# A new order of all words in an attention-and-gMLP kernel whose schedule is written out by hand

## The chip, the cores and the metric

One Trainium2 chip, one core of it. The time is what the device takes for one execution, in microseconds (us); the profile is one more execution, recorded by the hardware profiler. Engines: PE is TensorE (matmuls; PEld its weight loads), DVE is VectorE, ACT is ScalarE, POOL is GpSimd, SP is SyncE, which here only issues DMAs. A DMA can be issued from SP, ACT or POOL.

## The reference

Attention over 8 batches, 12 heads, 448 positions, head size 64, with q and k normalised by their root mean square, then a gMLP block on the joined heads (768 columns, 1024 hidden):

```python
q_n, k_n = rmsnorm(q, g_q), rmsnorm(k, g_k)
scores = q_n @ k_n.T / sqrt(64)
attn = softmax(scores)
x = (attn @ v) joined over heads          # [8, 448, 768]
h = relu(x @ w_in)                        # [8, 448, 1024]
u, w = h[..., :512], h[..., 512:]
w_n = (w - mean(w)) / sqrt(var(w) + 1e-6) # over the 512
w_s = w_spatial @ w_n + b_spatial         # over the 448 positions
out = (u * w_s) @ w_out                   # [8, 448, 768], float32
```

## The kernel before

The work is cut into words, and one text, `PLAN`, gives the order of all of them by hand. A loop at the end of the kernel reads the text word by word and calls `op_<letter>`. Each engine runs its own words in the order in which they stand, and waits for what another engine has to give. No scheduler changes this order. A word is a name with numbers, then after a slash the numbers of the buffers or PSUM banks it takes, then after a second slash the engine: `a` ACT, `v` DVE, `g` POOL, `s` SP. `E.4.1/c` is the exponential of group 4, unit 1, into buffer 12. PSUM has 8 banks for all uses; `SLOTS` gives the number of the other buffers (10 `raw` for loads, 22 `et`, 5 `os` for output rows).

A group G is four heads of one batch, so a batch has three groups (24 in all), each with seven units. The words in the order of the data:

- `L` loads q (0), k (1) or v (2) of a group, 448 KB, on SP; `l` loads halves of group 0; `gl` the two gains. `w`, `ws`, `wo`, `wb` load the weights, on POOL; `x` copies `w_in` with its rows swapped.
- `Q` squares (ACT, DVE or POOL), `R` sums (DVE), `I` and `J` make 1/rms (ACT), `N` multiplies (POOL or DVE); `q r i j n` are the same for the halves of group 0. `F` casts v.
- `P` and `p` transpose on TensorE and `K`, `k` copy the result from PSUM (DVE or ACT); for groups 6 and up `T` transposes by DMA instead, and `Z` scales k on DVE.
- `S` (L499) makes the scores of a unit on TensorE, eight matmuls on tiles of 64x32 of the array, into two banks; `E` (L507) takes their exponential on ACT.
- `s`, `a`, `b` (L534) are passes over the exponentials: the sums, and the two halves of the product with v; four matmuls of 64x32 for one group, eight when the word does two groups. `D` and `d` invert the sums on ACT, `X` (L563) writes the normalised result on DVE.
- `V` (L579) and `W` (L594) make the gate half of the hidden layer, `c` is its relu; `B`, `M`, `m`, `A` normalise it. `U` (L632) and `u` make the other half. `H` (L647) is the spatial product, `G` (L654) multiplies the halves, `O` (L663) is the output product, `o` (L354, L356) copies it from PSUM, `t` (L679, L681) stores it. `t` of the last 64 rows of two batches (m = 3) stores the pair.
- `z` (L247) is idle work: n matmuls on an identity, whose result nobody reads.

Words of DVE and POOL that read or write large tiles of SBUF go through `port`: each waits for the last such word of the other of the two engines.

Of the kernel before, what the change touches and what calls it, by code (L numbers as in the profile page):

```python
# [27 lines left out]
K.1.1/1/v P.2.0/6 K.2.0/1/v P.1.0/2 K.1.0/2/v s.0.2.0/3 E.0.0/4 S.0.3/45 E.0.3/5 S.0.2/67 E.0.2/6 F.0//g a.0.6.0/0  # L28
N.2.1/3 Q.3.0/1/v s.0.6.0 s.0.3.0 a.0.3.0 a.0.2.0 S.1.4/12 E.1.4/7 Q.4.0/0/v F.1//v s.0.0.0 S.1.6/45 E.1.6/8 S.1.0/67
a.0.1.0 E.1.0/9 S.1.5/12 E.1.5/a S.1.2/45 E.1.2/b R.3.0 P.2.1/6 s.0.4.0 S.1.1/12 E.1.1/c b.0.1.0/7 b.0.4.0 L.7.0/3  # L30
a.0.0.0 s.0.5.0 S.1.3/45 E.1.3/d a.0.4.0 R.4.0 K.2.1/2/v wo w.0 a.0.5.0 s.0.1.0 S.2.6/12 b.0.3.0 s.1.0.0/6 E.2.6/e
Q.3.1/2 R.3.1 I.3 J.3 Q.4.1/1 R.4.1 a.1.3.0/4 b.0.5.0 a.1.1.0 s.1.2.0 I.4 S.2.1/12 E.2.1/f Q.5.0/0 a.1.6.0 s.1.1.0
L.2.2/8 L.5.1/5 L.6.1/0 Y.4/5 s.1.6.0 N.3.1/0/v N.3.0/1/v S.2.0/12 s.1.4.0 s.1.3.0 b.0.6.0 s.1.5.0 L.3.2/9 J.4 N.4.0/2
N.4.1/3 D.0/0 b.1.5.0/3 b.1.6.0 E.2.0/g y.4//v L.7.1/6 a.1.2.0 d.0 S.2.3/12 D.1/1 R.5.0 P.3.1/5 P.3.0/6 K.3.1/3/v
K.3.0/3/v E.2.3/h Y.1/1 y.1//v Y.0/2 y.0//v S.3.4/56 d.1 Q.6.0/2/a a.1.0.0 E.3.4/i a.1.4.0 b.1.0.0 S.3.6/12 E.3.6/j
b.0.2.0 S.3.1/56 E.3.1/k X.0.0 P.4.1/0 Q.5.1/1/v K.4.1/0/v b.1.1.0 S.2.2/12 b.1.4.0 b.1.3.0 E.2.2/l R.5.1 L.4.2/7
S.3.3/56 E.3.3/0 b.0.0.0 b.1.2.0 a.1.5.0 w.1 I.5 X.1.1 X.1.0 Y.2/0 X.0.1 y.2//v S.2.5/12 E.2.5/6 P.4.0/3 K.4.0/0/v
S.3.5/56 E.3.5/2 Y.3/4 y.3//v L.8.0/4 S.3.2/12 Q.6.1/0 R.6.1 F.2//g J.5 R.6.0 E.3.2/8 s.2.1.1/70 s.2.6.1 s.2.3.1
s.2.5.1 F.3//g S.3.0/56 a.2.1.1/34 a.2.6.1 S.2.4/12 L.5.2/8 s.2.2.1 a.2.3.1 E.3.0/9 E.2.4/1 a.2.2.1 s.2.0.1 Q.7.1/1
R.7.1 Q.7.0/0/a R.7.0 N.5.0/0 a.2.5.1 a.2.0.1 S.4.4/56 E.4.4/3 s.2.4.1 b.2.2.1/12 N.5.1/1 a.2.4.1 b.2.3.1 b.2.1.1  # L40
D.2/1 b.2.0.1 b.2.4.1 b.2.5.1 Q.8.0/2 P.5.0/5 K.5.0/2/v L.8.1/9 L.9.1/2 P.5.1/6 K.5.1/1/v I.6 D.3/0 J.6 N.6.1/3 x.2
L.9.0/5 d.2 X.2.0 V.0.2.1/7 I.7 T.6.1/0 V.0.1.1/0 N.6.0/2 T.6.0/3 d.3 b.2.6.1 S.4.1/56 V.0.1.0 V.0.2.0 X.2.1 E.4.1/c
V.0.1.2 Q.9.1/1/a X.3.1 S.5.1/56 E.5.1/7 X.3.0 S.4.0/12 E.4.0/d V.0.2.2 c.0.2//v c.0.1//v R.9.1 V.0.0.1/3 J.7 L.10.0/0
U.0.0.1/4 S.4.6/56 E.4.6/4 S.5.3/12 x.0 U.0.2.2/7 L.11.1/1 B.0.2 Q.8.1/0 U.0.0.2 V.0.0.0 F.5//g E.5.3/5 N.7.0/0/v
Z.6/3/v S.5.2/56 S.5.0/01 E.5.0/b R.8.1 N.7.1/1 T.7.1/1 U.0.0.0 U.0.1.1/2 U.0.1.2 R.8.0 u.0.0//v E.5.2/a S.4.5/01
E.4.5/8 U.0.1.0 S.6.4/56 E.6.4/l U.0.2.1 S.4.3/01 I.8 E.4.3/0 V.0.0.2 u.0.1//v c.0.0//v S.4.2/56 F.4//g Q.9.0/1
E.4.2/h J.8 N.8.1/3 U.0.3.0/4 U.0.3.2 S.5.5/01 E.5.5/f S.5.6/23 E.5.6/k B.0.1 R.9.0 U.0.2.0 U.0.3.1 s.4.0.1/56
S.5.4/01 u.0.3//v E.5.4/9 L.10.1/8 u.0.2//v s.4.2.1 s.4.1.1 T.7.0/1 s.4.6.1 S.6.3/23 E.6.3/g N.8.0/2 s.4.5.1 s.4.3.1
s.4.4.1 D.5/1 b.4.5.1/47 a.4.1.1/01 a.4.0.1 Z.7/2/v a.4.4.1 a.4.5.1 a.4.2.1 a.4.3.1 a.4.6.1 D.4/0 S.6.6/23 b.4.2.1
b.4.6.1 T.8.1/0 d.5 X.5.0 d.4 X.4.0 L.7.2/3 L.6.2/6 T.8.0/0 E.6.6/1 I.9 b.4.1.1 b.4.4.1 b.4.3.1 b.4.0.1 X.5.1 X.4.1  # L50
Q.11.1/0/a S.7.5/56 S.7.3/01 J.9 E.7.3/i V.1.0.0/2 E.7.5/2 V.1.1.2/3 Q.10.0/2 W.0/7 c.0.3//a L.12.1/7 L.11.0/9
Q.10.1/1 S.7.6/01 E.7.6/6 S.7.2/45 E.7.2/e V.1.1.1 V.1.2.1/6 R.11.1 R.10.1 V.1.2.0 B.0.0 V.1.2.2 S.7.0/01 B.0.3
N.9.1/1 T.9.1/1 N.9.0/0 L.15.1/4 L.10.2/2 L.13.0/5 M.0 m.0 Z.8/0/v A.0.3 A.0.0 A.0.2 A.0.1 S.7.4/45 T.9.0/2 V.1.1.0
V.1.0.2 V.1.0.1 E.7.0/j H.0.1/0 c.1.1//a E.7.4/8 c.1.2//a R.10.0 I.10 c.1.0//a H.0.2/1 G.0.2 H.0.3/3 c.1.3//v G.0.3
F.7//a L.12.0/3 S.7.1/45 E.7.1/f S.6.2/12 J.10 Q.11.0/0 F.6//g L.9.2/6 E.6.2/a B.1.2 N.10.0/3 H.0.0/6 G.0.0 L.13.1/0
U.1.1.0/7 U.1.1.1 U.1.1.2 S.6.1/34 E.6.1/h G.0.1 S.6.5/12 u.1.1//a E.6.5/4 S.6.0/56 E.6.0/k O.0.0.1/0 B.1.3 Z.9/1/v
B.1.1 O.0.2.1/3 o.0.2.1/0/a O.0.0.0/4 O.0.2.0/7 o.0.0.1/1/v R.11.0 o.0.2.0//v Q.12.1/1/a U.1.2.2/1 S.9.1/56 I.11 J.11
S.8.0/23 E.8.0/7 B.1.0 R.12.1 Q.15.1/2/a U.1.3.1/0 F.10//g N.10.1/2 T.10.1/0 Q.13.0/0 E.9.1/c O.0.1.0/7 U.1.3.0
U.1.2.0 o.0.0.0//v U.1.3.2 u.1.3//v Q.12.0/1/v M.1 m.1 A.1.2 A.1.3 o.0.1.0/2/v U.1.2.1 U.1.0.2/2 U.1.0.1 U.1.0.0
u.1.2//a u.1.0//a O.0.1.1/3 o.0.1.1//a S.8.5/45 E.8.5/3 x.1 A.1.0 s.6.1.1/06 F.9//v A.1.1 S.9.6/12 E.9.6/9 s.6.0.1  # L60
R.12.0 R.13.0 s.6.3.1 s.6.2.1 N.11.1/1 s.6.5.1 s.6.6.1 s.6.4.1 S.8.2/34 E.8.2/0 Q.13.1/1 H.1.0/7 G.1.0 H.1.1/5 H.1.2/1
D.6/1 S.9.5/23 N.11.0/0 a.6.3.1/40 G.1.2 I.12 D.7/0 G.1.1 J.12 d.6 E.9.5/5 d.7 H.1.3/6 G.1.3 a.6.0.1 N.12.0/2 S.8.4/12
a.6.2.1 E.8.4/b a.6.1.1 a.6.4.1 R.15.1 R.13.1 S.8.1/56 E.8.1/d a.6.6.1 O.1.3.1/7 o.1.3.1/3/v S.9.3/12 b.6.6.1/35
E.9.3/1 b.6.4.1 b.6.2.1 T.10.0/1 L.8.2/2 a.6.5.1 X.7.0 F.8//g N.12.1/3 b.6.0.1 I.13 b.6.5.1 X.6.0 S.8.3/67 b.6.3.1
S.9.4/12 E.9.4/6 b.6.1.1 L.15.0/8 L.12.2/6 O.1.3.0/0 o.1.3.0//v X.6.1 X.7.1 J.13 E.8.3/8 O.1.0.0/4 o.1.0.0/4/a
O.1.0.1/1 o.1.0.1//v S.9.2/67 E.9.2/l Q.15.0/0 s.8.4.1/20 Z.10/2/v L.14.1/1 S.9.0/34 s.8.5.1 s.8.1.1 b.8.5.1/51
s.8.3.1 b.8.1.1 S.8.6/67 E.9.0/a E.8.6/e s.8.2.1 b.8.2.1 b.8.4.1 S.10.1/34 s.8.0.1 b.8.3.1 Q.14.1/2 E.10.1/j t.0.0
T.11.0/3 L.13.2/9 b.8.0.1 L.14.0/3 R.15.0 T.11.1/1 N.13.1/0/v Z.11/3/v s.8.6.1 a.8.5.1/67 a.8.6.1 a.8.0.1 a.8.4.1
D.9/1 F.13//g T.12.1/0 L.16.0/2 t.1.3 b.8.6.1 Q.14.0/1 a.8.1.1 L.16.1/7 D.8/0 a.8.3.1 T.13.1/1 a.8.2.1 S.10.5/34 d.9
X.9.0 d.8 X.8.0 E.10.5/k V.2.1.0/0 V.2.2.1/2 V.2.1.1 L.11.2/0 L.19.1/9 S.11.1/67 E.11.1/2 I.15 J.15 N.15.0/1 V.2.0.1/3  # L70
T.12.0/2 X.9.1 X.8.1 V.2.0.0 S.10.4/45 E.10.4/4 L.15.2/8 S.10.0/67 E.10.0/g V.2.0.2 R.14.1 R.14.0 V.2.1.2 c.2.1//v
c.2.0//v O.1.1.1/1 Q.16.0/0/a S.11.4/45 S.11.0/67 E.11.0/i E.11.4/f I.14 o.1.1.1/1/v V.2.2.0 V.2.2.2 U.2.0.0/0
N.13.0/3/v L.19.0/5 T.13.0/0 Z.13/1/v c.2.2//v U.2.0.1 S.10.6/67 E.10.6/h Z.12/0/v U.2.3.1/3 N.15.1/0 L.17.0/4 R.16.0
S.10.3/45 E.10.3/3 F.11//g S.11.3/12 E.11.3/5 Q.16.1/2/v F.12//v S.11.5/67 E.11.5/7 J.14 U.2.0.2 U.2.3.2 F.15//g
O.1.2.0/4 U.2.3.0 u.2.3//a S.10.2/12 S.12.5/56 E.12.5/a Q.17.0/1 N.14.1/2 N.14.0/3 O.1.2.1/7 o.1.2.1/3/v U.2.2.1/3
U.2.2.0 U.2.1.2/5 E.10.2/6 o.1.2.0//v u.2.0//v S.11.6/12 B.2.2 E.11.6/b S.11.2/67 E.11.2/9 R.16.1 B.2.1 U.2.1.1
U.2.1.0 u.2.1//v U.2.2.2 u.2.2//v S.13.3/01 E.13.3/e s.10.5.1/42 s.10.0.1 S.12.1/67 s.10.2.1 s.10.4.1 E.12.1/c
# [643 lines left out]
```

## Time and profile before

| | us |
|---|---|
| median of 3 runs | 274.83 |
| lowest, highest | 273.71, 276.78 |
| the profiled execution, whole | 274.1 |
| its span, first to last instruction | 272.2 |
| TensorE busy | 256.3 |
| ACT busy | 215.8 |
| DVE busy | 212.2 |
| POOL busy | 120.9 |

Mean granted clock of TensorE 0.994. The profile's page gives busy times, 40 slices of the span, the DMA queues, the chain of work that ended last, the costliest groups of instructions, and the DMA issues. More closely the trace answers by stages, by groups, by waits and by a timeline. A group's row reads: line, engine, operation, what it writes and reads with shapes, count, busy time, mean of one in ns, idle time before them and what ended it. A timeline's row reads: start, length, engine, line, operation, count.

### The profile page before, as it was taken

Reading aid. Unit: us, or ns where it says so; the run is one execution under the profiler, and the core shown is the slowest. Engines: PE = TensorE matmul, PEld = TensorE weight load, DVE = VectorE, ACT = ScalarE, POOL = GpSimd, SP = SyncE. Lnnn points to the kernel's source line nnn. Section 1 sums busy time; section 2 is a strip of 40 time slices with the busy share of each in tenths; the row PEclk is TensorE's granted clock in tenths of the full one; section 3 lists DMA queues with packets and bytes.
Section 4 is the critical chain, followed back from the end, with each engine's and each line's share of the span. In section 5 each row is a group of like instructions: output and inputs, shape, how many; then the busy total and the mean of one; then the engine's idle time right before and its main releaser. Section 6 shows DMA issues by size and latency. Waiting matters only on the chain.

```text
span 272.2 us, 9903 instructions
## 1 busy us (share of the span) xinstructions
PE 256.3 (94%) x4243; PEld 126.7 (47%) x4262; DVE 212.2 (78%) x385; ACT 215.8 (79%) x353; POOL 120.9 (44%) x92
## 2 busy tenths in 40 slices
PE   7898988999999998999999999999999999999992
...
PEclk9979999999999999999999999999999999999999
...
GB/s 251 315 302 352 259 351 296 210 237 266 213 330 221 261 290 251 258 336 240 301 178 354 183 243 190 211 198 67 118 164 91 60 2 60 2 116 152 83 213 192
DMA packets 59235, 57.27 MB, mean 210 GB/s; under 512 B 35448, under 2 KB 54840, under 8 KB 59192
## 3 DMA queue, kind: packets, MB, share of 16 engines
...
q8 instruction: 33, 0.54, 0.8%
...
q14 instruction: 10, 0.08, 0.1%
...
## 4 chain that ended last, share of the span: by engine, by line
PE 69%; DMA 8%; DVE 8%; ACT 5%; issue 3%; POOL 1%; SPq 0%; DVEq 0%
PE ps L534 14%; PE ps L663 12%; PE ps L632 12%; PE ps L499 11%; PE ps L579 9%; PE ps L647 8%; DMA raw<-in_k_dram 6%; ACT et L507 3%; DMA out_dram<-os 2%; PE ps L594 2%; DVE s L607 1%; DVE ss L386 1%; DVE gt L654 1%; DVE xt L563 1%; POOL nrm L419 1%
## 5 line engine op out<-in xcount | busy, mean ns | idle before, releaser
L507 ACT ACTIVATE et<-ps 128x896 bf16<-128x896 f32 x168 | 146.1, 920 | 16.0 <-PE ps L499 14.7
L419 POOL TENSOR_TENSOR nrm<-raw,rs 128x896 bf16<-128x896 f32 x32 | 53.7, 1689 | 33.9 <-DVE nrm L419 10.9
L499 PE MATMUL ps<-qT,kT 64*32 64x448 bf16 x1344 | 60.1, 355 | 3.9 <-ACT et L507 1.8
L375 POOL TENSOR_TENSOR sqt<-raw 128x896 f32<-128x896 f32 (+1 forms) x28 | 46.0, 1652 | 19.4 <-DVE sqt L375 5.8
L534 PE MATMUL ps<-et,vt 64*32 64x448 bf16 x1344 | 48.2, 350 | 1.2 <-issue 0.8
L386 DVE TENSOR_REDUCE ss<-sqt 128x14 f32<-128x896 f32 x46 | 48.4, 1075 | 0.5 <-ACT sqt L373 0.4
L663 PE MATMUL ps<-w_out,gt 128*128 128x384 bf16 x224 | 42.5, 326 | 0.1
L499 PEld LDWEIGHTS <-kT 64*32 64x32 bf16 x1344 | 20.8, 89 | 34.7 <-issue 25.1
L563 DVE TENSOR_TENSOR xt<-ps,rc 128x448 bf16<-128x448 f32 x48 | 27.5, 617 | 11.1 <-PE ps L534 7.4
L663 PEld LDWEIGHTS <-gt 128*128 128x128 bf16 x224 | 21.0, 98 | 18.7 <-issue 4.1
L534 PEld LDWEIGHTS <-vt 64*32 64x32 bf16 x1344 | 22.7, 92 | 14.9 <-issue 5.2
L647 PE MATMUL ps<-w_spT,vs 128*128 128x448 bf16 (+1 forms) x128 | 28.1, 353 | 0.2 <-DVE vs L623 0.2
L534 PE MATMUL ps<-et,ones 64*32 64x448 bf16 x672 | 26.7, 350 | 0.0
L304 POOL CAST vt<-raw 128x896 bf16<-128x896 f32 x16 | 14.8, 931 | 25.6 <-PE ps L534 11.9
L632 PE MATMUL ps<-xt,w_in 128*128 128x448 bf16 x104 | 26.0, 353 | 0.0
L354 ACT ACTIVATE os<-ps 128x384 f32<-128x384 f32 x25 | 12.3, 498 | 17.1 <-PE ps L663 10.6
L607 DVE BATCH_NORM_STATS2 s<-vs 128x6 f32<-128x512 bf16 (+1 forms) x32 | 21.9, 685 | 2.7 <-ACT vs L570 2.2
L356 DVE COPY os<-ps 128x384 f32<-128x384 f32 x31 | 16.9, 549 | 8.5 <-PE ps L663 6.9
L654 DVE TENSOR_TENSOR gt<-ps,us 128x448 bf16<-128x448 f32 (+2 forms) x48 | 20.0, 458 | 3.9 <-PE ps L647 1.6
L632 PE MATMUL ps<-xt,w_in_x 128*128 128x448 bf16 x88 | 22.3, 353 | 0.1
L579 PE MATMUL ps<-w_in,xt 128*128 128x512 bf16 x70 | 20.1, 381 | 0.6 <-issue 0.5
L579 PEld LDWEIGHTS <-xt 128*128 128x128 bf16 x144 | 12.2, 98 | 17.0 <-issue 6.9
...
## 6 DMA issues: line engine op xcount, KB each, us to landing
...
out_dram<-os SPq DMA_DIRECT2D x24, 384.0 KB, 3.3
...
out_dram<-os SPq DMA_DIRECT2D x8, 192.0 KB, 4.4
w_out<-in_moe_w_out_dram POOLq DMA_DIRECT2D x1, 768.0 KB, 12.1
```

Of the source, the lines that this page charges most:

```text
L375: port(eng, eng.tensor_tensor(out=t, in0=x, in1=x, op=ALU.mult))
L386: dve.tensor_reduce(out=sss[G % 3][:, i].rearrange("p r c -> p (r c)"), in_=sqt[where.pop(("sq", G, i))].rearrange("p r (c d) -> p (r c) d ...
L419: port(eng, eng.tensor_tensor(out=nrm[sl[0]].rearrange("p c r d -> p r c d"), in0=raw[where["raw", G, i]].rearrange("p r (c d) -> p r c d" ...
L499: pe.matmul(out=ps[at:at + 32, sl[n], 0:S], lhsT=kT[64 * r:64 * r + 64, c, 64 * hh + 32 * x:64 * hh + 32 * x + 32], rhs=qT[64 * r:64 * r + ...
L507: act.activation(out=ets[sl[0]].rearrange("p n (t c) -> p n t c", c=C), in_=ps[:, a:b + 1:b - a, 0:S].rearrange("p n (c t) -> p n t c", c= ...
L534: pe.matmul(out=ps[to:to + 32, where[kind, G][0], 0:S], lhsT=w, rhs=et_of(G, r, c)[at:at + 64], start=(n == 1), stop=(n == C), tile_positi ...
L563: dve.tensor_tensor(out=xts[b % 2][:, 2 * g + half, :], in0=ps[:, where.pop(("ab"[half], G))[0], 0:S], in1=rcs[where["rc", G]], op=ALU.mult)
L579: pe.matmul(out=ps[:, bank, :], lhsT=xts[b % 2][:, j, 128 * m:128 * m + 128], rhs=w_of(b, j)[:, DH:], start=(n == 1 and j == 2 * g), stop= ...
L607: dve.bn_stats(out=s6, in_=vss[b % SLOTS["vs"]][rows, m, :])
L632: pe.matmul(out=ps[:, bank, 0:S], lhsT=w_of(b, j)[:, 128 * f:128 * f + 128], rhs=xts[b % 2][:, j, :], start=(n == 1 and j == 2 * g), stop= ...
L647: pe.matmul(out=ps[:, sl[0], 0:S], lhsT=vns[b % SLOTS["vs"]][rows, m, 128 * f:128 * f + 128], rhs=w_spT[rows, n, :], start=(m == 0), stop= ...
L663: pe.matmul(out=ps[:, sl[0], 0:384], lhsT=gt[:, f, at:at + 128], rhs=w_out[:, f, 384 * h:384 * h + 384], start=(f == 0), stop=(f == 3))
```

## The change

All words stand in a new order with new buffers and banks; the count of most is the same. What differs in the words:

- `gl` is issued from ACT, not SP. The first z stays (22 matmuls), the four later ones (9 matmuls in all) go. Twelve words of a new kind, `h`, take places in the first part of the order.
- `N`: 38 on POOL and 8 on DVE, before 32 and 14. `F`: 21 on POOL, 3 on DVE, before 16 on POOL, 6 on DVE, 2 on ACT. `Q`: 24 on POOL, 9 on DVE, 13 on ACT, before 27, 6, 13. `c`: 11 on ACT and 21 on DVE, before 15 and 17. `o`: 28 and 28, before 25 on ACT and 31 on DVE. `u`: 14 on ACT, before 13. `k`: two on ACT, before one.
- `t` with m = 3 is one DMA for the pair of batches; before it was two. `t` may take a half (384 of the 768 columns); the eight stores of the last batch are halves, four issued from SP and four from ACT.

```diff
 PLAN = """
-l.1.0/0 setup l.0.0/1/a q.1.0/0/v r.1.0 q.0.0/1/v l.1.1 gl.0//s gl.1//s r.0.0 l.0.1//a q.0.1//a r.0.1 q.1.1//g r.1.1
-gA z.22/7 gB/0 L.2.0/2 i.0 j.0 n.0.0//v p.0.0/1 gC L.1.0/3 Q.2.0/2/a R.2.0 i.1 j.1 Q.1.0/1/a R.1.0 L.1.1/4 L.2.1/5
-Q.1.1/0/a R.1.1 Q.2.1/2/a L.3.0/6 L.4.0/7 L.0.2/8 w.2 L.3.1/9 n.1.1//g I.1 J.1 z.2/2 p.1.1/2 n.0.1//g L.6.0/1 z.1/4
-p.0.1/3 k.0.1/0/v k.1.1/0/a R.2.1 I.2 k.0.0//v n.1.0//g p.1.0/4 k.1.0//v z.5/5 S.0.4/56 ws L.1.2/0 N.1.1/0 S.0.5/23
-J.2 N.2.0/1/v E.0.5/0 S.0.0/01 E.0.4/1 z.1/4 S.0.6/23 E.0.6/2 S.0.1/45 E.0.1/3 P.1.1/7 N.1.0/2/v wb L.4.1/4 L.5.0/2
...
-o.6.0.0/0/a t.6.2 o.6.0.1//a t.6.0 G.7.1 O.7.0.0/3 O.7.0.1/5 O.7.1.1/2 o.7.0.1/2/a o.7.0.0//v t.7.0 o.7.1.1/1/v
-O.7.1.0/1 o.7.1.0//a t.7.1 O.7.2.0/4 o.7.2.0/4/a O.7.2.1/7 o.7.2.1//v t.7.2 O.7.3.0/6 o.7.3.0/3/v O.7.3.1/0 o.7.3.1//a
-t.7.3
+setup l.1.0/0 l.1.1 q.1.0/0/v r.1.0 l.0.0/1/a q.0.0/1/g r.0.0 gl.0//a gl.1//a z.22/7 h.0/0 h.0/1 L.1.0/2 q.1.1//g
+l.0.1//a i.0 j.0 n.1.0//g gA L.1.1/3 L.2.0/4 p.1.0/2 gB/3 q.0.1//a r.1.1 r.0.1 L.2.1/5 Q.1.0/2/a R.1.0 i.1 Q.1.1/0/a
+gC h.0/4 h.1/5 n.0.0//g p.0.0/6 h.0/7 j.1 n.1.1//g n.0.1//g R.1.1 L.7.1/6 h.0/0 L.4.0/7 Q.2.0/1/a k.1.0/0/v I.1 R.2.0
+p.1.1/1 p.0.1/4 Q.2.1/2/a R.2.1 k.1.1//v h.0/3 h.1/5 h.0/7 h.0/0 L.3.1/8 J.1 N.1.1/0 N.1.0/1/v k.0.0/0/a S.0.1/23
+L.0.2/9 k.0.1//a S.0.5/56 S.0.2/01 I.2 J.2 N.2.0/2/v L.3.0/0 E.0.1/0 h.0/7 E.0.5/1 P.1.1/4 E.0.2/2 F.0//v P.1.0/7
+K.1.0/1/v S.0.0/23 E.0.0/3 S.0.4/56 E.0.4/4 S.0.3/01 E.0.3/5 N.2.1/3 K.1.1/1/v L.5.0/1 L.1.2/3 L.4.1/2 P.2.0/7
...
+u.7.1//a H.7.0/2 G.7.0 H.7.3/3 t.5.2 G.7.3 H.7.1/4 G.7.1 t.6.1 O.6.2.1/5 O.6.2.0/1 o.6.2.1/3/v o.6.2.0//v O.7.1.1/7
+o.6.0.0//a t.6.0 o.7.1.1/2/a t.7.1.1 t.6.2 O.7.1.0/6 o.7.1.0//a t.7.1.0//a O.7.3.1/0 o.7.3.1/0/v t.7.3.1 O.7.0.1/2
+o.7.0.1/1/v t.7.0.1 O.7.2.0/3 o.7.2.0/4/a t.7.2.0//a O.7.3.0/4 o.7.3.0//v t.7.3.0//a O.7.0.0/5 o.7.0.0//v t.7.0.0
+O.7.2.1/1 o.7.2.1//a t.7.2.1//a
...
+    def op_h(sl, e, r):
+
+        at = slice(64 * r, 64 * r + 64)
+        for _ in range(2):
+            pe.matmul(out=ps[0:32, sl[0], 0:S].rearrange("p (c t) -> p c t", c=C), lhsT=ident[at, 0:32],
+                      rhs=ident[at, None, 0:T].to_broadcast([64, C, T]), start=True, stop=True, tile_position=(64 * r, 0))
...
-    def op_t(sl, e, b, m):
+    def op_t(sl, e, b, m, *half):
         t = oss[where["os", b, m]]
-        assert where["o", b, m, 0] and where["o", b, m, 1]
+        cols = slice(384 * half[0], 384 * half[0] + 384) if half else slice(0, DM)
+        assert all(where["o", b, m, h] for h in half or (0, 1))
         eng = engines[e or "s"]
         if m == 3:
-            for n in range(2):
-                eng.dma_start(out=out[b - 1 + n, TAIL:S], in_=t[64 * n:64 * n + 64])
-            return
-        eng.dma_start(out=out[b, 128 * m:128 * m + 128], in_=t)
+            eng.dma_start(out=out[b - 1:b + 1, TAIL:S, cols], in_=t[:, cols])
+        else:
+            eng.dma_start(out=out[b, 128 * m:128 * m + 128, cols], in_=t[:, cols])
```

220 lines of the change are left out of this document (109 added, 111 removed).

## The prediction

> **What bounds the kernel now.** The page first: its span, the engines' busy time, the slices, the chain that ended last. Then one view by stages (`start:end length`, then busy time and count of each engine, granted clock, DMA share, GB/s).
>
> ```profile
> span 272.2 us, 9903 instructions
> PE 256.3 (94%) x4243; PEld 126.7 (47%) x4262; DVE 212.2 (78%) x385; ACT 215.8 (79%) x353; POOL 120.9 (44%) x92
> PE   7898988999999998999999999999999999999992
> PEclk9979999999999999999999999999999999999999
> PE 69%; DMA 8%; DVE 8%; ACT 5%; issue 3%; POOL 1%; SPq 0%; DVEq 0%
> ...
> 0.00:4.00 4.00, 2.32 (x7) 0.99 (x8) 1.48 (x10) 1.28 (x1) 0.70 (x6) 1.00 0.54 166
> 4.00:14.50 10.50, 9.37 (x71) 4.59 (x69) 9.94 (x16) 7.18 (x14) 7.03 (x8) 1.00 1.04 325
> 14.50:50.60 36.10, 31.96 (x691) 18.41 (x692) 30.27 (x42) 32.76 (x50) 26.64 (x21) 0.95 1.06 305
> 50.60:100.00 49.40, 48.91 (x828) 23.10 (x830) 44.39 (x81) 46.27 (x78) 36.04 (x25) 1.00 1.09 256
> 100.00:200.00 100.00, 96.77 (x1767) 45.35 (x1760) 84.08 (x147) 91.55 (x150) 48.86 (x34) 1.00 0.94 220
> 200.00:267.30 67.30, 67.01 (x909) 34.31 (x911) 42.00 (x93) 36.35 (x63) 1.62 (x1) 1.00 0.31 100
> 267.30:272.20 4.90, 0.00 (x0) 0.00 (x0) 0.00 (x0) 0.44 (x1) 0.00 (x0) 0.99 0.51 161
> ```
>
> From 50.6 to 267.3 us TensorE is busy 212.7 of 216.7 us; behind it lie 4.9 us of last copy and store. Before 50.6 no engine is full: ACT idles 3.3 us between 14.5 and 50.6, DVE 5.8, and DMA is at a share above 1. So the kernel has three parts: a start that feeds TensorE too slowly, a long stretch in which TensorE's own work is the bound, a short tail. "Busy" is too coarse for the middle, because the ends of matmuls are modelled; I priced the work by how fast matmuls follow each other. The chain gives that (start, length, line, count):
>
> ```profile
> 260.72 6.51 PE ps L663 x40
> 227.84 2.46 PE ps L534 x104
> 252.92 0.76 PE ps L647 x4
> 198.17 0.76 PE ps L632 x4
> 163.58 0.97 PE ps L579 x4
> 67.20 1.42 PE ps L594 x12
> 17.18 2.42 PE L438 MATMUL ps<-ident,nrm 128*128 128x128 bf16 x21
> ```
>
> Output matmuls (L663) follow at 0.163 us; L647 and L632 at 0.19; L579 at 0.216 (0.97 less 0.09 for a change of shape, below, over 4); L594 gives 1.3 us for 12. The 64x32 matmuls of L534 run eight at a time on eight places of the array: 104 are 13 rounds in 2.46, 0.19 a round; an S word (L499) is one such round of eight. The transposes (L438) took 0.115 each here, at half clock, so 0.057 at full. Over the whole order, counted in the PLAN: O 224 x 0.163 = 36.5; S and passes 168 + 269 rounds x 0.19 = 82.6; U 192 x 0.19 = 36.3; H 128 x 0.19 = 24.2; V 144 x 0.216 = 31.1; W 4 x 1.3 = 5.2; P, p and Y about 6.6. Together 222.5 us.
>
> The order also makes TensorE change the shape of its array, from 128x128 to tiles of 64x32 and back:
>
> ```profile
> 151.99 1.69 PE L647 MATMUL ps<-w_spT,vs 128*128 128x448 bf16 x8
> 153.61 0.57 PE L499 MATMUL ps<-qT,kT 64*32 64x448 bf16 x16
> 154.11 0.82 PE L663 MATMUL ps<-w_out,gt 128*128 128x384 bf16 x4
> 154.77 0.92 PE L647 MATMUL ps<-w_spT,vs 128*128 128x448 bf16 x4
> 155.62 0.38 PE L534 MATMUL ps<-et,vt 64*32 64x448 bf16 x8
> ```
>
> Read the starts. From L663 to L647, one shape, 0.66 us pass: four matmuls at 0.163, and nothing more. From L647 to the tiled L534 0.85 pass where four at 0.19 need 0.757: the change cost 0.09. From eight L647 to L499: 1.62 against 1.51, again 0.1. Two rounds of L499 to L663: 0.50 against 0.38, 0.12. I take 0.093, the usual excess over the trace. The order before has 161 such changes (counted where neighbouring PE words differ in shape): 15.0 us. With 222.5 this makes 237.5 us of work; the last matmul ends at 267.2, so **29.7 us are lost**. By 50.6 us the words then done sum to 30 us: 20.6 are lost in the start, 9 in the 217 us after it.
>
> **The change, part by part.** The words are the same but for a few; S, passes, V, U, H, O, P, X and T all keep their numbers. What differs is the order, so I counted it in both PLANs.
>
> *Changes of shape* fall from 161 to 136. Only those count that lie where TensorE is full: from the first V word on they fall from 133 to 107. 26 x 0.093 = **-2.4 us**. TensorE hides nothing here, as it is itself the bound; ends -2.4 and, if part of it turns into waits, -1.
>
> *The start.* Before the first E word ACT has 7.4 us of work in the old order and 8.4 in the new (both k words of k on ACT, L455, one more of 1.0 us). What it then does:
>
> ```profile
> 14.53 2.54 ACT L507 ACTIVATE et<-ps 128x896 bf16<-128x896 f32 x3 [0.30 <-PE ps L499]
> 17.29 1.73 ACT L507 ACTIVATE et<-ps 128x896 bf16<-128x896 f32 x2 [0.21 <-PE ps L499]
> 20.31 0.92 ACT L507 ACTIVATE et<-ps 128x896 bf16<-128x896 f32 x1 [1.30 <-PE ps L499]
> ...
> 12.60:16.10 3.50, 2.34 (x37) 0.78 (x36) 3.47 (x5) 2.99 (x5) 2.62 (x3) 0.99 1.06 287
> 16.10:19.50 3.40, 3.40 (x29) 2.29 (x26) 1.98 (x3) 2.70 (x4) 1.34 (x2) 0.50 1.17 286
> ...
> 48.37 2.20 DVE L563 TENSOR_TENSOR xt<-ps,rc 128x448 bf16<-128x448 f32 x4
> ```
>
> The 1.30 us before the sixth E is S waiting behind three P words at half clock (the 2.42 us of L438, 1.2 us more than at full). In the new order DVE's and ACT's squares of the first two pairs of loads stand ahead of the weights (w words come after 13 E words instead of before the first), so I expect the first E again at about 14.5: the extra 1.0 us on ACT sits in idle time that ACT has before 14.5 (10.5 - 7.18 = 3.3 us). From there to the four X words of groups 2 and 3 (here 48.37 to 50.57) the order has 36.8 us of ACT work before and 34.6 after, by the mean durations of the page's groups, and the same 42 us of DVE work. ACT took 32.76 busy us for its 36.8, so 34.6 take 30.8; with 2 us idle instead of 3.3 the X words are done at 14.5 + 32.8 = 47.3 by ACT. DVE, 40 busy us (9.94 + 30.27) from 4.0 on, ends at 48 with some 4 us of idle time where it now has 6. I take 48: 2.6 earlier. But the new order has by then two V words instead of five, 3 x 0.432 = 1.3 us less TensorE work done. What counts is the time lost: **-1.3 us**. Ends: -4.1 (X at 45.2, by ACT without idle), and +3 (X at 50.6 as now, and two half-clock stretches instead of one, 1.3 each, in the start). The loads have slightly more lead, counted in the PLANs: from the freeing of a raw buffer to the first use of what is loaded lie 16.0 us of TensorE work on average, 15.1 before.
>
> The idle words h (12, each two 64x32 matmuls, at most 0.38 us) stand where TensorE waits for k, K or P; z falls from 31 matmuls to 22. Cost nothing while the wait lasts longer; if all delayed, 12 x 0.38 = 4.6.
>
> The half-clock stretch lasted some 3.4 us (0.50 in the row from 16.10), after 3.5 us in which TensorE had been busy 2.34. [...]
>
> *Work moved between engines.* Six N words go from DVE to POOL, five F words to POOL, three Q leave it:
>
> ```profile
> L419 POOL TENSOR_TENSOR nrm<-raw,rs 128x896 bf16<-128x896 f32 x32 | 53.7, 1689 | 33.9 <-DVE nrm L419 10.9 <-ACT rs L404 10.8 <-DVE kT L457 6.2
> L419 DVE TENSOR_TENSOR nrm<-raw,rs 128x896 bf16<-128x896 f32 x14 | 14.9, 1084 | 1.3 <-POOL sqt L375 1.3
> ```
>
> POOL gets some 12 us more (6 x 1.69 and the F words), DVE some 7 less, ACT 1.3 less. POOL has 120.9 of 272 and nothing after 200 us, so this costs nothing unless a DVE word that waits for POOL by the order on their port (`port`) holds up the A, G and X words queued behind it on DVE; POOL and DVE take turns 54 times instead of 46, 8 more waits of at most 1.7 us, with DVE 16% idle in 100 to 200 as cover. I take 0, ends -1 and +1.5.
>
> *The tail.*
>
> ```profile
> 267.25 0.49 ACT L354 ACTIVATE os<-ps 128x384 f32<-128x384 f32 x1 [1.41 <-PE ps L663]
> 267.77 1.11 SPq L679 DMA_DIRECT2D out_dram<-os  x2
> out_dram<-os SPq DMA_DIRECT2D x24, 384.0 KB, 3.3
> out_dram<-os SPq DMA_DIRECT2D x8, 192.0 KB, 4.4
> ```
>
> Now the last copy is followed by two issues on SP, 1.11 us, and the second one's store ends the kernel. In the change the last copy on ACT is followed by one issue on ACT's own queue: **-0.5 us**. A store of half the bytes landed no sooner (4.4 against 3.3), so I count nothing for the halves; eight stores of 192 KB in the last 5.2 us of TensorE work are 300 GB/s, which the start's 305 to 325 shows possible. Ends -1.1 and +1. ACT issues four of the stores between its copies; the only one that waits for DVE (t.7.3.0) stands two O words before the last copy, 1.3 us, so the copy is not held. The tails in one store save four issues on SP, which waits for copies most of its time at the end: nothing.
>
> *The sum*: -2.4 - 1.3 - 0.5 = -4.2. The profiled execution took 274.1 us, 1.9 beside its span of 272.2; 274.1 - 4.2 = 269.9. The median of the runs shown is 274.83, 0.7 above that execution; I put the forecast between, **270.2 us**. Without changes in the start it would be 271.5.
>
> **The rivals.** Less than about 1% can't be told from no change here (the three runs spread over 1.1%): the bounds are 272.1 and 277.6.
>
> *The start gives nothing.* DVE, not ACT, paces it, and its work is the same 42 us; X then comes at 50 to 50.6, and the 1.3 us of V words not yet done are lost: 269.9 + 2.6 = 272.5. For it: DVE at 84% there. Against: much of its idle time was waiting for transposes at half clock and for loads that now come earlier. 17%.
>
> *The clock.* TensorE at half clock through the whole thin start, four stretches of 3.4 us, where the forecast has none: 4 x 1.3 = 5.2, so 275.1; with two, 272.5. It would also be the case in which the idle words don't do what they say. For it: h uses a small tile and its rounds are few. Against: before, with nine z matmuls after the first 22, there was one. 8%.
>
> *TensorE waits for banks: slower.* Fewer changes of shape mean that S words come two and three in a row and then give way to longer runs of other work; ACT, 91.6% busy between 100 and 200 us, must empty the pairs of PSUM banks for them.
>
> ```profile
> PE ps L499 <- ACT et L507: 1.8, 5, 0.6
> 105.26 0.83 issue
> ```
>
> Such a wait cost 0.36 us on average (1.8 by 5). It decides against the change from 13 of them on (4.65 us); with 16, 5.8, it is 275.7 to 276. Against it: counted in the PLANs, of the banks that an S used last 68 are written again within 1.6 us of TensorE work before and only 44 after. 10%.
>
> *More than forecast*: the start at its end of -4.1, so 267.1; 8%. The forecast's own case has 57%.
>
> **How the numbers follow.** The forecast's own range, from the ends that don't add up all at once, is 267.5 to 272.8. With 8% below it at 267.1 and the first and second rival at 272.5, the range is 266.8 to 274.6; beyond it are the four-stretch clock and the waits. Faster by over 1%: nearly all of the 57%, the 8% and a third of the 17%, 0.70; within 1%: 0.22; slower: the worst of the bank waits and of sums of ends, 0.08. [...]
>
> **What would show it.** Right: in the stages view the X words of groups 2 and 3 by 48 us, TensorE full from then on, 4.4 us or less after the last matmul, and the last matmul near 263.5. The changes of shape show as gaps of 0.09 at each place where L499 or L534 meets another line. Wrong: E words on ACT with idle before them from L499 beyond 2 us in the first 50; half-clock stretches after 10 us; waits of L499 for L507 of more than 4 us in all; idle time of A or X on DVE behind POOL; a last store that lands over 4 us after its issue.

## The result: 289.1 us against 275.2, slower by 5%

The median of four runs is 289.13 us (288.73 to 290.26) where the kernel before took 275.20 beside it (273.71 to 276.78). The ratio is 1.051, 95% interval 1.044 to 1.058. The forecast was 270.2, with a range up to 274.6: outside, and on the other side.

**The page of the changed kernel**: its span, the busy times, three rows of the slices (TensorE's busy share, its clock, what the DMAs moved), and the chain that ended last.

```profile
span 288.5 us, 9935 instructions
PE 260.6 (90%) x4277; PEld 129.4 (45%) x4277; DVE 208.9 (72%) x376; ACT 214.7 (74%) x352; POOL 132.4 (46%) x102
PE   7988997999999999499999999998699999999920
PEclk9999997999999999979999999999799999999985
GB/s 251 384 361 263 220 185 132 280 221 272 303 289 229 156 324 77 152 287 282 302 326 166 220 253 246 161 315 62 230 157 59 2 5 55 55 59 124 253 185 37
...
PE 25%; DMA 5%; SPq 1%; DVE 1%; issue 0%; ACT 0%; ACTq 0%; DVEq 0%
```

New are holes: TensorE at 4 tenths in slice 17 (115 to 122 us), at 6 in slice 29 (202 to 209), nearly empty for the last two. Most of the rest looks as it did. The clock falls behind these holes and once before them, in slice 7. In slice 16, just ahead of the first hole, and in slice 28, around 200 us, the DMAs move only 77 and 62 GB/s. The chain breaks off early, so TensorE's 25% can't be compared with the 69% before; its 5% for DMAs are transposes by DMA.

**The stages** (columns as in the prediction: busy and count of PE, PEld, DVE, ACT, POOL, then clock, DMA share, GB/s):

```profile
14.50:50.60 36.10, 31.17 (x652) 17.72 (x657) 30.70 (x41) 31.78 (x50) 24.57 (x22) 0.95 0.91 233
47.10:50.60 3.50, 3.47 (x26) 2.07 (x34) 2.58 (x4) 0.06 (x1) 2.23 (x2) 0.51 0.86 234
100.00:125.00 25.00, 21.10 (x369) 9.52 (x367) 17.97 (x29) 19.48 (x33) 16.61 (x12) 0.94 1.09 172
196.00:202.00 6.00, 5.20 (x47) 2.27 (x45) 2.70 (x6) 5.60 (x10) 0.93 (x1) 1.00 0.13 52
200.00:225.00 25.00, 21.89 (x503) 11.26 (x509) 14.15 (x31) 19.84 (x31) 6.90 (x6) 0.93 0.55 133
275.10:288.50 13.40, 0.59 (x4) 0.14 (x2) 0.54 (x1) 0.49 (x1) 0.00 (x0) 0.66 0.35 90
280.00:286.90 6.90, 0.00 (x0) 0.00 (x0) 0.00 (x0) 0.00 (x0) 0.00 (x0) 0.50 0.13 48
```

Read the DMA share in the row from 196 and in the last row: 0.13 is 2/16. For six and for seven microseconds the DMA engines did the work of two of sixteen, and moved 52 and 48 GB/s. From 280 to 286.9 us nothing else ran: the kernel's end waits for two engines. Before, the last matmul was followed by 4.9 us; now by 13.4.

**What those two engines were doing** shows in SP's timeline around 190 us and ACT's at the end (start, length, engine, line, operation; an issue of a DMA has the length for which it held its queue). L686 is the store of a pair's tails, L481 a transpose by DMA, L464 the DVE word that scales its result, L506 the scores on TensorE:

```profile
189.23 0.59 SPq L686 DMA_DIRECT2D out_dram<-os  x1
189.95 8.52 SPq L481 DMA_TRANSPOSE kr<-nrm  x1
...
203.53 1.25 SPq L481 DMA_TRANSPOSE qT<-nrm  x1
203.86 0.45 DVE L464 TENSOR_SCALAR kT<-kr,g_col 128x896 bf16<-128x896 bf16 x1 [5.08 <-DMA kr<-nrm]
204.37 1.10 PE L506 MATMUL ps<-qT,kT 64*32 64x448 bf16 x8 [3.11 <-DVE kT L464]
275.45 0.62 ACTq L686 DMA_DIRECT2D out_dram<-os  x1
276.12 0.49 ACT L361 ACTIVATE os<-ps 128x384 f32<-128x384 f32 x1 [1.14 <-PE ps L670]
```

The store of a pair is issued at 189.23. The transpose behind it holds SP for 8.52 us, where an undisturbed one holds it 1.25 (203.53). Its data come 13.8 us after the issue; DVE idles 5.08 us for it, TensorE 3.11 for DVE. The store at 103.33 does the same to what follows it, and the one at 275.45 sets the kernel's end. Its semaphore has three records, at 276.49, 286.31 and 286.82 us, where a store of 64 rows in the kernel before has sixteen. The store issued behind it, at 276.64, has fourteen of its sixteen records by 280.45 and the last two at 286.79 and 287.32, as fits two engines that still work on the pair.

Behind the store at 103.33 it is a load that comes late, and program text:

```profile
105.08 12.84 SPq L481 DMA_TRANSPOSE kr<-nrm  x2
115.78 3.32 POOL L382 TENSOR_TENSOR sqt<-raw 128x896 f32<-128x896 f32 x2 [4.25 <-DMA raw<-in_q_dram]
117.50 1.09 DVE L393 TENSOR_REDUCE ss<-sqt 128x14 f32<-128x896 f32 x1 [5.25 <-POOL sqt L382]
120.41 0.38 PE L506 MATMUL ps<-qT,kT 64*32 64x448 bf16 x7 [2.89 <-issue]
121.79 1.04 PE L670 MATMUL ps<-w_out,gt 128*128 128x384 bf16 x4 [1.01 <-DVE os L363]
q14 instruction: 2, 0.02, 3.3%
122.20:125.70 3.50, 3.50 (x25) 1.12 (x24) 2.44 (x5) 1.85 (x4) 3.43 (x3) 0.51 1.20 186
204.20:207.60 3.40, 3.23 (x66) 1.57 (x74) 3.27 (x7) 1.50 (x2) 3.17 (x3) 0.50 1.18 287
```

A load of q is issued at 104.12, just behind the store. Fourteen of its sixteen semaphore records are there by 108.36 us; the last two come at 115.20 and 115.65, after the store's last record (114.56). POOL idles 4.25 us for this load, DVE 5.25 us for POOL, and TensorE's output matmuls (L670) wait until 121.79 for a copy that DVE makes later. In the middle of an S word TensorE also waits 2.89 us for nothing that the profile shows (`issue`). That wait lies inside the other one, so it need not have cost anything by itself. The sixth row is one of two queues that bring program text, between 105 and 120 us: 2 packets, 0.02 MB, 3.3% of 16 engines' time in 15 us, which is 7.9 us; one of them, of 8 KB, took 7.53. Whose text it is the trace doesn't say, so it is not shown that this packet is what TensorE waited for. The last two rows are what comes behind each hole: TensorE at half clock for 3.4 us. The clock fell after the waits, not before them.

**Two engines, and an outer dimension of 2.** The new store writes `out[b - 1:b + 1, TAIL:S, cols]`: its outer dimension is the pair of batches, of size 2. On its semaphore stand one early record and two late ones, for the last pair at 276.49, 286.31 and 286.82 us, and in the two stretches above the DMA share is 0.13. The two stores that stood there before wrote 64 rows from 64 partitions each; they have sixteen records each. That the number of engines follows the outer dimension was the author's estimate from these two forms; it is what the experiments put to the test.

### The profile page after: what moved, and what is told of

Read it like the earlier page. It is cut to its first block, busy times and chain, and to the rows that moved or that the text cites. A ratio compares the mean times of both kernels' runs of the same rounds, so it can differ in the third digit from the quotient of the medians.

```text
span 288.5 us, 9935 instructions
## 1 busy us (share of the span) xinstructions
PE 260.6 (90%) x4277; PEld 129.4 (45%) x4277; DVE 208.9 (72%) x376; ACT 214.7 (74%) x352; POOL 132.4 (46%) x102
## 3 DMA queue, kind: packets, MB, share of 16 engines
q10 hardware_dynamic: 858, 1.25, 1.3%
## 5 line engine op out<-in xcount | busy, mean ns | idle before, releaser
L514 ACT ACTIVATE et<-ps 128x896 bf16<-128x896 f32 x168 | 145.8, 923 | 20.8 <-PE ps L506 19.7
L426 POOL TENSOR_TENSOR nrm<-raw,rs 128x896 bf16<-128x896 f32 x38 | 63.7, 1688 | 29.7 <-ACT et L514 10.1
L506 PE MATMUL ps<-qT,kT 64*32 64x448 bf16 x1344 | 60.5, 358 | 7.7 <-DVE kT L464 3.5
L382 POOL TENSOR_TENSOR sqt<-raw 128x896 f32<-128x896 f32 (+1 forms) x26 | 41.9, 1622 | 22.4 <-DMA raw<-in_q_dram 5.8
L670 PE MATMUL ps<-w_out,gt 128*128 128x384 bf16 x224 | 41.6, 327 | 1.0 <-DVE os L363 1.0
L506 PEld LDWEIGHTS <-kT 64*32 64x32 bf16 x1344 | 21.7, 91 | 37.0 <-issue 23.9
L311 POOL CAST vt<-raw 128x896 bf16<-128x896 f32 x21 | 19.2, 930 | 24.2 <-DVE vs L630 9.3
L670 PEld LDWEIGHTS <-gt 128*128 128x128 bf16 x224 | 21.4, 98 | 18.3 <-issue 3.5
L541 PE MATMUL ps<-et,ones 64*32 64x448 bf16 x672 | 27.9, 364 | 0.4 <-issue 0.3
L541 PEld LDWEIGHTS <-vt 64*32 64x32 bf16 x1344 | 21.8, 93 | 14.2 <-issue 3.2
L654 PE MATMUL ps<-w_spT,vs 128*128 128x448 bf16 (+1 forms) x128 | 27.6, 353 | 0.1
L661 DVE TENSOR_TENSOR gt<-ps,us 128x448 bf16<-128x448 f32 (+2 forms) x48 | 20.2, 461 | 10.0 <-PE ps L654 4.9
L586 PE MATMUL ps<-w_in,xt 128*128 128x512 bf16 x78 | 22.7, 393 | 0.2 <-DVE xt L570 0.2
L361 ACT ACTIVATE os<-ps 128x384 f32<-128x384 f32 x28 | 13.2, 490 | 9.9 <-PE ps L670 6.3
L363 DVE COPY os<-ps 128x384 f32<-128x384 f32 x28 | 15.4, 552 | 4.6 <-PE ps L670 2.4
```

The costliest lines, as they stand in the source:

```text
L382: port(eng, eng.tensor_tensor(out=t, in0=x, in1=x, op=ALU.mult))
L426: port(eng, eng.tensor_tensor(out=nrm[sl[0]].rearrange("p c r d -> p r c d"), in0=raw[where["raw", G, i]].rearrange("p r (c d) -> p r c d" ...
L506: pe.matmul(out=ps[at:at + 32, sl[n], 0:S], lhsT=kT[64 * r:64 * r + 64, c, 64 * hh + 32 * x:64 * hh + 32 * x + 32], rhs=qT[64 * r:64 * r + ...
L514: act.activation(out=ets[sl[0]].rearrange("p n (t c) -> p n t c", c=C), in_=ps[:, a:b + 1:b - a, 0:S].rearrange("p n (c t) -> p n t c", c= ...
L541: pe.matmul(out=ps[to:to + 32, where[kind, G][0], 0:S], lhsT=w, rhs=et_of(G, r, c)[at:at + 64], start=(n == 1), stop=(n == C), tile_positi ...
L586: pe.matmul(out=ps[:, bank, :], lhsT=xts[b % 2][:, j, 128 * m:128 * m + 128], rhs=w_of(b, j)[:, DH:], start=(n == 1 and j == 2 * g), stop= ...
```

## The experiments

The theory was: the outer dimension of 2 costs everything beyond the forecast, and the rest of the change is worth about what was forecast. The rivals: the new order itself waits (banks, loads, the start), or one store for two batches is bad in any form. Each ratio below is against runs of the kernel before that were taken beside it; their medians lie between 275.2 and 276.4 us.

**Two stores again, in the new order.**

```diff
-            eng.dma_start(out=out[b - 1:b + 1, TAIL:S, cols], in_=t[:, cols])
+            for n in range(2):
+                eng.dma_start(out=out[b - 1 + n, TAIL:S, cols], in_=t[64 * n:64 * n + 64, cols])
```

> The changed kernel with one thing undone: the rows of the pair of batches (m = 3) go out again in two DMAs of 64 rows each, whole and half tiles alike. Theory E (engines): a store whose outer dimension is the pair, 2 rows of [64, cols], runs on two of the 16 DMA engines, as the changed kernel's rows of 50 GB/s at a DMA share of 0.13 show (0.13 is 2 of 16), and everything later in those two engines' rings waits for it. Then the 5.5 us lost at 117 to 125 us, the 4.5 us at 204 to 210 and the 8.5 us of longer tail go: 288.5 - 18.5 = 270 us of span, 271 to 273 us in all, and no row of the trace has a share of 0.13 at 50 GB/s. Theory H (halves): the long tail comes from eight half stores, four of them issued from ACT; then 13 us still lie behind the last matmul and the time stays above 282. Theory O (order): transposes wait 8 to 14 us because of where the new order puts them; then the stalls at 117 and 204 stay and the time is 278 or more.

Measured: 270.94 us (268.29 to 271.27), ratio 0.981 [0.973, 0.988]. Stages of this kernel:

```profile
100.00:200.00 100.00, 99.57 (x1836) 48.29 (x1821) 86.51 (x154) 91.54 (x150) 65.27 (x45) 1.00 1.01 251
263.60:269.50 5.90, 1.00 (x7) 0.39 (x4) 0.85 (x2) 0.49 (x1) 0.00 (x0) 0.89 0.58 193
```

TensorE is busy 99.57 of 100 us at full clock: the holes and the half clock are gone together. One line, beside 1650 words in a new order, was worth 18.2 us (289.13 less 270.94), and the new order without it is faster than the old, by 1.2 to 2.7%.

**One store, in the old order.** The same line the other way round, in the kernel before: `out[b - 1:b + 1, TAIL:S]` from the whole tile.

> The kernel before with this one thing of the change: the pair's rows in one DMA (four such stores in all). Theory E: the last store, 393 KB over two engines at 50 GB/s, takes 7.9 us where two stores land 2.3 us after their issue, so the tail grows from 4.9 to 10.5 or 11.5 us; the three others hold up what is behind them by 0 to 5 us each: 281 to 290 us. Theories H and O: nothing of theirs is in this kernel; 274 to 276 us.

Measured: 294.65 us (294.3 to 296.7), ratio 1.071 [1.065, 1.078]: 19.1 us lost against the 275.54 beside it, more than expected. Its stage from 100 us, DVE's row and the half clock behind it:

```profile
100.00:125.00 25.00, 18.38 (x299) 7.54 (x283) 13.61 (x20) 15.33 (x25) 9.43 (x7) 0.86 1.17 200
118.07 0.45 DVE L457 TENSOR_SCALAR kT<-kr,g_col 128x896 bf16<-128x896 bf16 x1 [6.41 <-DMA kr<-nrm]
117.10:123.90 6.80, 4.72 (x32) 1.64 (x39) 4.04 (x6) 1.95 (x4) 2.56 (x2) 0.50 1.16 288
```

So the loss belongs to the store and not to the order it stands in. Here too it comes through what is issued behind the store: a transpose behind the one at 102.40, for which DVE waits 6.41 us.

**Two stores, but split by columns**: each again over both batches, half of the columns. It has the number of issues of the good form and the outer dimension of the bad one.

```diff
-            eng.dma_start(out=out[b - 1:b + 1, TAIL:S, cols], in_=t[:, cols])
+            w2 = (cols.stop - cols.start) // 2
+            for n in range(2):
+                part = slice(cols.start + w2 * n, cols.start + w2 * n + w2)
+                eng.dma_start(out=out[b - 1:b + 1, TAIL:S, part], in_=t[:, part])
```

> Two DMAs per pair again, but cut by columns: each reaches over both batches, so either has the pair as its outer dimension. Theory E: two engines each, and the same two, so nothing is won: 287 to 292 us, 12 us or more behind the last matmul. If it is the number of stores that counts: 270 to 273 us.

Measured: 290.69 us (two runs, 289.24 and 292.14), ratio 1.057 [1.049, 1.065]. The stage of its first hole with TensorE's longest wait, at 120.42, and DVE's longest for a transpose, at 203.60:

```profile
100.00:125.00 25.00, 20.88 (x352) 9.39 (x351) 16.70 (x27) 19.19 (x32) 16.78 (x12) 0.89 1.05 229
PE ps L670 <- DVE os L363: 4.1, 1, 4.1
DVE kT L464 <- DMA kr<-nrm: 5.0, 1, 5.0
```

The holes are nearly those of one store, the first of them without an `issue` wait. The number of stores is not the cause.

**The rows of each store cut into 2 and into 4 parts**, to get other numbers of engines: `.rearrange("(x t) c -> x t c", x=2)` on each of the two stores, and with 4.

> As the kernel with two stores, but each store's 64 rows are written as 2 x 32, so the outer dimension of either DMA is 2 again. Nothing else differs: same bytes, same addresses, same number of DMAs. Theory E: two engines each, and both DMAs on the same two, so the same 128 rows in the same time: 286 to 291 us, as with one store, with rows of 50 GB/s at a share of 0.13. If it was the joining of the two batches in one DMA, and not the outer dimension: 271 to 273 us.

> The same with the 64 rows written as 4 x 16: outer dimension 4. Theory E: four engines, about 100 GB/s and a share of 0.25 while such a store runs alone, half the time of each: the tail some 4 us shorter than with two engines and the stalls at 117 and 204 small: 274 to 280 us. If the number of engines does not follow the outer dimension: as the kernel with two stores.

Measured: 270.23 us, 0.981 [0.973, 0.989], and 270.10 us, 0.981 [0.972, 0.989]. Neither tells anything of the number of engines: the parts lie end to end in memory, and in the traces their DMAs have the same 64 rows as the two stores of the first experiment. They stand as two repeats of the first experiment. The dependence on the outer dimension therefore rests on 2 against 64 alone.

**One store whose outer dimension is 64.** The two tails of a pair are written row by row in turn into `gt`, so that partition 2t+n holds row t of batch n, and one store takes the pair.

```diff
-        for to, t in ((0, slice(0, S)),) if b % 2 == 0 else ((S + T, slice(0, TAIL)), (S, slice(TAIL, S))):
-            dve.tensor_tensor(out=gt[:, f, to:to + t.stop - t.start], in0=ps[:, bank, t], in1=u[:, t], op=ALU.mult)
+        both_ = gt[:, f, TAIL:TAIL + 2 * T].rearrange("p (t n) -> p t n", n=2)[:, :, b % 2]
+        at = (S + T) * (b % 2)
+        dve.tensor_tensor(out=gt[:, f, at:at + TAIL], in0=ps[:, bank, 0:TAIL], in1=u[:, 0:TAIL], op=ALU.mult)
+        dve.tensor_tensor(out=both_, in0=ps[:, bank, TAIL:S], in1=u[:, TAIL:S], op=ALU.mult)
...
-            eng.dma_start(out=out[b - 1:b + 1, TAIL:S, cols], in_=t[:, cols])
+            eng.dma_start(out=out[b - 1:b + 1, TAIL:S, cols].rearrange("n t c -> t n c"), in_=t[:, cols])
```

> The two runs with the 64 rows split into 2 x 32 and 4 x 16 came out as the kernel with two stores, and their DMAs stand in the trace with the same shape as its own (64 rows): the split was merged away, so they said nothing of theory E. This run keeps one store per pair, with the pair as an inner dimension: the rows of the two batches lie interleaved over the partitions (row t of batch n at partition 2t + n; the G words write the last 64 columns with stride 2, in 16 more DVE instructions), so the store's outer dimension is 64 rows. Theory E: 16 engines, no row of 50 GB/s at a share of 0.13, 269 to 272 us. If one store that reaches into two batches is slow by itself: 286 to 291 us.

Measured: 268.44 us (268.10 to 268.96), ratio 0.976 [0.973, 0.979]: faster than both kernels, and a little below the range expected. Stages and the last issues on ACT:

```profile
14.50:50.60 36.10, 32.22 (x711) 17.95 (x705) 32.54 (x45) 33.23 (x52) 25.68 (x22) 1.00 0.95 251
50.60:75.00 24.40, 24.25 (x405) 10.60 (x403) 20.95 (x36) 22.74 (x37) 15.99 (x12) 1.00 1.09 268
100.00:200.00 100.00, 99.82 (x1886) 48.72 (x1878) 86.51 (x161) 91.99 (x150) 65.03 (x45) 1.00 0.98 245
261.40:266.40 5.00, 0.59 (x4) 0.14 (x2) 0.54 (x1) 0.49 (x1) 0.00 (x0) 0.83 0.52 193
...
261.32 0.69 ACTq L688 DMA_DIRECT2D out_dram<-os  x1
262.06 0.49 ACT L361 ACTIVATE os<-ps 128x384 f32<-128x384 f32 x1 [1.49 <-PE ps L672]
```

With an outer dimension of 64 one store for a pair of batches was as good as two (268.44 us against 270.94), and the sixteen more pieces of DVE work cost nothing that shows. At the end ACT issues the last pair store in 0.69 us and copies at once. With two stores (the first experiment) two issues stand there, and the copy starts behind the second:

```profile
263.93 1.40 ACTq L687 DMA_DIRECT2D out_dram<-os  x2
265.37 0.49 ACT L361 ACTIVATE os<-ps 128x384 f32<-128x384 f32 x1 [2.19 <-DMA out_dram<-os]
```

**The same store in the old order**, to see what it is worth by itself (the same words in `op_G`, and one store of the whole tile).

> The order of before, with one store for the tails of a pair whose outer dimension is the 64 rows, not the 2 batches (G writes the two tails row by row in turn). If the 2 in the store's outer dimension made the loss, nothing of the 19.5 us that one store with an outer dimension of 2 cost in this order is left: 275.2 us as before, between 272.5 and 276.5, no stretch at half clock after 50 us, and the last store 0.5 us earlier because one issue stands behind the last copy where two stood. If one store for a pair is bad in any form, it is above 285. If the 2.5 us by which this store was ahead of two stores in the new order came from the store, it is 272.7.

Measured: 276.36 us beside 276.43 for the kernel before, ratio 0.999 [0.995, 1.003]. The form of the store gains nothing there, as expected; of the two kernels with one store in the old order, one loses 19.1 us and the other none.

**Whole tiles instead of halves for the last batch** (with two stores per pair).

> The kernel with two stores, with the last batch stored by whole tiles (one word per 128 rows, two of its four on ACT's queue), to measure the tail by itself. The prediction took 0.5 us for the changed tail, and in the kernel with two stores it was 0.1 (5.9 us behind the start of the last O word, 6.0 in the kernel before). If the halves help: 0.3 to 0.8 us longer behind the last matmul than with halves. If they do nothing: within 0.2. In time 269.5 to 271.5 either way.

Measured: 271.31 us (271.04 to 273.54), ratio 0.989 [0.983, 0.995]. Its end:

```profile
261.98 1.20 ACTq L686 DMA_DIRECT2D out_dram<-os  x2
263.22 0.49 ACT L360 ACTIVATE os<-ps 128x384 f32<-128x384 f32 x1 [2.00 <-PE ps L669]
263.74 0.77 ACTq L688 DMA_DIRECT2D out_dram<-os  x1
```

From the last issue to the end of the span (269.3) pass 5.6 us, against 3.6 with halves (265.89 to 269.5). Halves do land sooner here, by about 2 us in these profiles; the medians differ by 0.4 us only and don't tell it.

**The start.** In the changed kernel TensorE waits 2.1 us near 46 us for transposes whose input POOL makes, and POOL stands in the squares of a load, L.7.0, that has not landed. I moved these squares and their sum behind other words, and the swapped copy `x.2` out of SP's way (two stores per pair).

```diff
-J.5 Q.7.1/2 R.7.1 Q.7.0/0 R.7.0 S.3.0/01 ... N.6.0/3 d.2 ... V.0.2.1 I.7
+J.5 Q.7.1/2 R.7.1 S.3.0/01 ... N.6.0/3 Q.7.0/0 d.2 ... V.0.2.1 R.7.0 I.7
```

> The kernel with two stores, with three words moved. There POOL's square of q of group 7 stands ahead of the norm of k of group 5 and waits for its load, and the transposes of group 5 on TensorE wait for that norm: 1.5 us lost at 47.5 us, the step by which the start came out later than predicted. Q.7.0 now follows the norms of groups 5 and 6, R.7.0 stands before I.7, and x.2 (which waits on SP for a weight load until 45 us, with five loads queued behind it) follows those loads. If that chain is the cause: no wait of the transposes on POOL over 0.5 us, the time lost by 50 us 1 to 2 us less, 268 to 270 us. If DVE or ACT set the pace there: the same 270 to 271 us.

Measured: 271.42 us (270.07 to 273.59), ratio 0.987 [0.983, 0.991]: no gain over the first experiment. Its waits between 44 and 56 us:

```profile
ACT ls L407 <- DVE ss L394: 3.5, 1, 3.5
PE ps L640 <- ACT et L515: 3.1, 1, 3.1
DVE ss L394 <- POOL sqt L383: 2.5, 1, 2.5
```

The wait went down the chain: POOL squares later, DVE sums later, ACT stands 3.5 us in the logarithm of that sum (`I.7`, which I had not moved), and TensorE waits 3.1 us for the exponentials queued behind it on ACT.

So I moved the whole chain, the two ACT words too (`Q.7.0` behind N.6.0, `R.7.0` behind E.5.6, `I.7` behind E.4.0, `J.7` behind V.0.0.1; one interleaved store).

> The new order with one interleaved store (268.4 us), and the whole chain that waits for the load L.7.0 moved later on every engine: its squares behind N.6.0 on POOL, its sum (R.7.0) behind E.5.6, its two ACT words (I.7 and J.7) behind E.4.0 and the V words of that place; x.2 behind L.9.1. If that load was the limit between 43 and 55 us and only moved the wait from POOL to DVE and ACT when the squares alone were moved, the lost time at 57 us is 1.5 to 2 us less (about 20 instead of 21.5 to 23) and the whole 266.5 to 267.3. If the loads as a whole are too slow there, or something later takes the wait, it stays at 268.4, within 0.7, and the lost time is the same by 75 us.

Measured: 268.56 us (267.51 to 269.46), ratio 0.973 [0.969, 0.976]; not told apart from 0.976 without the move. Stages:

```profile
14.50:50.60 36.10, 33.64 (x738) 18.20 (x730) 31.89 (x44) 34.59 (x53) 24.53 (x22) 1.00 1.00 271
50.60:75.00 24.40, 23.37 (x380) 10.42 (x379) 21.74 (x36) 22.04 (x37) 17.35 (x12) 1.00 0.99 239
```

By 50.6 us TensorE had 1.4 us more of work than in the kernel without the move (33.64 against 32.22); in the next 24 us 0.9 of it went again, in short waits at 54 to 58 us for copies from PSUM on DVE. The lost time (the table below says how it is counted) is 20.2 us at 56.4, as the first theory had it, but 25.1 at the last O word, against 24.7 without the move. The chain was a limit, and behind it stand others.

**Without the idle words** (one interleaved store, the twelve h words taken out).

> The new order with one interleaved store (268.4 us), without its twelve h words. If the idle words are what keeps TensorE's clock up in the start, a stretch of 3.4 us at half clock comes back in the first 50 us, as before had one, and costs 1.3 to 1.7 us: 269.7 to 270.1. If they do nothing for the clock and stand in time that TensorE waits anyway, it stays at 268.4, within 0.7; if they delayed words, it is lower by up to 1.

Measured: 269.13 us (268.80 to 269.32), ratio 0.975 [0.972, 0.978], not told apart from 0.976 with them. But the clock did what the first theory says. The first row is without the idle words, the second with them:

```profile
13.90:20.70 6.80, 6.51 (x89) 3.27 (x85) 5.43 (x9) 6.07 (x9) 3.79 (x5) 0.51 1.06 379
```
```profile
13.90:20.70 6.80, 6.28 (x111) 3.19 (x111) 6.55 (x9) 6.69 (x11) 3.79 (x4) 1.00 0.98 334
```

Two stretches of 3.4 us at half clock came back, where 1.3 to 1.7 us were expected to be lost. P.5.0 then began at 47.98 us instead of 47.61; in the seven profiles that have the same words up to there and the idle ones it began between 47.61 and 48.71, so no loss is shown. By this TensorE was not the bound in these microseconds.

## Why the prediction was wrong, step by step

**The step that failed** is the last of the tail: "The tails in one store save four issues on SP, which waits for copies most of its time at the end: nothing." It counted issues and bytes of the new store and not how its bytes lie. The bound given beside it, "eight stores of 192 KB in the last 5.2 us of TensorE work are 300 GB/s, which the start's 305 to 325 shows possible", came from loads at a DMA share above 1 (1.04 and 1.06); the new store had two engines, 48 to 52 GB/s. And it was counted in the tail alone, though two of the four pairs of batches are stored in the middle, at 103 and 189 us, with loads and transposes around them. None of the rivals named it.

To size the other steps I priced each TensorE word as the prediction did, each class now by its own mean over the trace, and took the time that passed less the work of the words done. "Lost" is that difference, in us, in one profile of each kernel:

| | work | lost at 50 | lost at the last O word | from there to the end | span |
|---|---|---|---|---|---|
| before | 238.7 | 20.4 | 27.6 | 6.0 | 272.2 |
| changed | 236.3 | 22.7 | 38.4 | 13.8 | 288.5 |
| two stores | 236.3 | 21.8 | 27.3 | 5.9 | 269.5 |
| one store, outer dimension 64 | 236.3 | 20.8 | 24.7 | 5.4 | 266.4 |

The changed kernel against the one with two stores is 19.0 us of span: 7.9 in the tail, 10.2 between 50 us and the last O word (the changed kernel loses 5.8 at 117 to 125 us and 5.2 at 204 to 210), and 0.9 in the start. The third pair's store, at 258.65, adds nothing between that can be told apart.

*Changes of shape*: right. -2.4 forecast, -2.4 in the priced work. The price holds in the new order too: in the middle of both kernels' traces, by the median of the starts, a change into the tiles costs 0.09 us and one out of them 0.12 to 0.13. Nothing of it came back as waits for banks.

*The start*: -1.3 forecast, +0.4 (outer dimension 64) and +1.4 (two stores) measured. The direction was wrong: seven profiles have the new start's words and three the old's, and priced alike by the prediction's prices each of the seven had lost more by 50.6 us than each of the three, by 0.3 to 2.9 us. The X words of groups 2 and 3, forecast for 48 us, were done at 51.1 and 52.1. The step took ACT's and DVE's work as the limit and set the X words by it; the limit was a chain from a late load through POOL. The moved chain showed it (1.4 us more of TensorE's busy time by 50.6 us) and that nothing of it remained by the end.

*Work between engines*: 0 forecast. POOL's 132 us cost nothing that shows from 50 us on, but the squares of L.7.0 on POOL belong to the chain above.

*The tail*: -0.5 forecast, -0.1 with two stores and -0.6 with the store of 64. "So the copy is not held" was wrong with two stores: they hold ACT's queue for 1.40 us, right up to the last copy. That the halves were counted at nothing was too little by what the profiles show, some 2 us from the last issue to the end.

*The middle*, which has no term of its own in the forecast, gained 1.7 us with two stores and 3.3 with the store of 64, by these profiles. The waits of TensorE between 50.6 and 261 us say what went; the first row is of before, the second of the kernel with two stores, each the largest there:

```profile
PE ps L579 <- issue: 1.9, 8, 0.8
```
```profile
PE ps L639 <- DVE us L579: 0.5, 1, 0.5
```

Eight waits for nothing that the profile shows, 1.9 us, have no like there. Such waits in this stretch come to 1.3 to 3.1 us in the three profiles of the old order and to at most 0.7 in those of the new, but for the one inside the hole at 117. What these waits were for, and why the new order had fewer, no run here shows. The size of the gain is not settled by one profile each: in the profile of the old order with the store of 64 the last O words start 4.3 us later than in that of the kernel before, with no more lost by 50 us. So 270.94 with two stores lies near the forecast's 270.2 by luck, and not by its terms: -2.4, +1.4, -1.7 and -0.1, where -2.4, -1.3, 0 and -0.5 were summed.

*The rivals*: the start gave nothing, as the first had it, and less. The clock fell behind the two new holes, and in the start from 47.1 to 50.6 us, behind a wait of 2.1 us for POOL; in four of the seven profiles with this start it did not fall there. Waits for banks did not come: L506 waited 0.9 us for ACT in all.
